# A decode block on one core: ScalarE sums the score products of 24 cache positions, and one weight load is split by partitions

## The chip, the cores and the metric

The kernel runs on one core of one Trainium2 chip. A core has a matrix engine (TensorE, in the profile PE), a vector engine (VectorE, DVE), a scalar engine (ScalarE, ACT), GpSimd (POOL), and SyncE (SP), which here issues nearly all transfers. Sixteen DMA engines move data between the chip's memory (HBM) and the core's own memory (SBUF, 128 partitions). The metric is the device time of one execution in microseconds (us), lower is better. Three runs of the kernel before took 662.41, 664.11 and 664.48 us, median 664.11.

## The reference

One decode step of a transformer block for two sequences, all inputs in bf16: layer norm of x, attention of 32 heads over a cache of 8192 keys and values of 128 numbers each, an output projection, a residual, layer norm again, and a gated ReLU feed-forward layer with a second residual.

```python
def _A_ref(x, k_cache, v_cache, wq, wo):
    q = (x @ wq) ...                                     # (B=2, 32 heads, 1, 128)
    scores = einsum("bhqd,bhkd->bhqk", q, k) * (128 ** -0.5)
    o = einsum("bhqk,bhkd->bhqd", softmax(scores), v)
    return (o as rows of 32*128) @ wo
def _B_ref(x, W_gate, W_up, W_down):
    gate = x @ W_gate; up = x @ W_up
    return ((gate * (gate > 0)) * up) @ W_down
h = A_x + _A_ref(_layernorm(A_x), A_k_cache, A_v_cache, A_wq, A_wo)
h2 = h + _B_ref(_layernorm(h), B_W_gate, B_W_up, B_W_down)
```

The two caches hold 268 MB of the 281 MB that the kernel reads. Each key and each value is used once, by one query.

## The kernel before

**Steps.** A step takes four heads of one sequence. There are 16 such groups: steps 0 to 14 (`Q` = `LASTQ` = 14 is the last full one), and the sixteenth is done as two half steps of two heads, `p0` and `p1`. The keys of a full step are one tile of 128 partitions by 32768 numbers (8 MB): 32 partitions per head, and on each partition 256 *positions* of 128 numbers. The values of a step are a tile of the same size.

**Buffers.** SBUF has three buffers of 8 MB (`bufs`). The keys of step i lie in buffer 2i mod 3, its values in the next. So the values of step i+1 are loaded into the buffer of the keys of step i, and the keys of step i+2 into the buffer of the values of step i. Keys and values alternate on SyncE's queue in the order K0, V0, K1, V1, K2 and so on, each issued when its buffer comes free; near the end the order is V12, K13, K14, V13, V14, then the half steps.

**Scores.** In a step the last `npe` positions go to TensorE (`scores_pe`, L309): it transposes them (L332), ScalarE copies the transposes back (L333), TensorE multiplies them by the query (L323), and small copies put the scores into the tile `scol` (L354). The first `nv = 256 - npe` positions go to VectorE: `products` (L358) multiplies the keys by the query in place with one instruction (L362), and `scores` (L366) halves the 128 products of each position four times by adding (L373), sums the remaining eight (L377) and takes the maximum over `scol` (L381). `npe` is 24 in steps 0 to 8, 32 in steps 9 to 13, and 16 from step 14 on (`NPE_AT`, L61).

**The rest of a step.** `largest` (L385) spreads the maxima by a TensorE product, `exponentials` (L390) takes the minimum of their negatives on VectorE (L393) and the exponentials on ScalarE (L398), and `values` (L405) multiplies 64 groups of four positions with the values on TensorE (L411); ScalarE copies the result out (L416).

**Order.** Nothing is scheduled by a tool. The program text is the order in which each engine takes its instructions, and an engine waits in that order; semaphores between engines are put in from the tiles that are read and written. In the loop (L477 to L509) a step issues `scores_pe`, `products`, `scores`, the load of the next values, `largest`, `exponentials`, then in some steps extra work, then `values` and the load of the keys after next. The extra work is `close(i - 1)` in steps 4, 8 and 12 (it divides the outputs of four finished groups by their sums, on TensorE and VectorE), and in step 12 also `lay_rows(0, ...)` (L496): two `spread` operations on VectorE (L446), two TensorE products of their results (L457) and a VectorE copy. The loads of the weights `wo`, `W_gate`, `W_up` and `W_down` come after step 14 (L519 to L561). Eight completion semaphores serve all loads in turn, so a load also waits until the load eight before it has landed.

**The tail.** After the last attention products the second layer norm and the feed-forward layer run on the weights as they land; the last instruction group is the product with `W_down` (L644), an addition, a transpose, and the 2 KB store of the result (L655).

Of the kernel before, what the change touches and what calls it, by code (L numbers as in the profile page):

```python
# [7 lines left out]
ACT = mybir.ActivationFunctionType  # L8
ALU = mybir.AluOpType
# [14 lines left out]
def kernel(  # L24
# [32 lines left out]
    VG = 4  # L57


    NPE = 32  # L60
    NPE_AT = {**{i: 24 for i in range(9)}, LASTQ: 16, LASTQ + 1: 16, LASTQ + 2: 16}  # L61
    QZ = 32


# [59 lines left out]
    class Step:  # L124
        def __init__(self, i):
            self.i = i
            self.quad = i <= LASTQ
            if self.quad:
                self.b, self.g = divmod(i, NQ)
                self.nh, self.nt = NH, TILE // Dh  # L130
                self.kt = bufs[0 if i == LASTQ else 2 * i % 3]
                self.vt = bufs[1 if i == LASTQ - 1 else (2 * i + 1) % 3]
                self.qr = qrep[:, i, :]
                self.pg, self.zc = pgq, zc[:, self.b, self.g, :]
            else:
# [8 lines left out]
            self.nv = self.nt - self.npe  # L144
            self.hp = P // self.nh

        def rows(self, j):
# [32 lines left out]
    with tc.manual_schedule():  # L180
# [123 lines left out]
            shares(i)  # L304
            normalise(i)

        scols = {}

        def scores_pe(s, between=lambda: None):  # L309


            U = s.npe // 4
            nh, nv = s.nh, s.nv
            row_ps = ps.tile([nh * U, 4 * P], f32, tag="row")

            def times_q(c0):
                for k in range(0, TPC, 4):
                    u = (c0 + k) // 4
                    if s.quad:
                        z = qz[:, QZ - NH - NH * u:QZ - NH - NH * u + NH * U]  # L320
                    else:
                        z = qzp[:, s.k, 14 - 2 * u:14 - 2 * u + 2 * U]
                    nc.tensor.matmul(  # L323
                        out=row_ps, lhsT=z, rhs=s.kt[:, (nv + c0 + k) * Dh:(nv + c0 + k + 4) * Dh],
                        start=(u == 0), stop=(u == U - 1),
                    )

            for c0 in range(0, s.npe, TPC):
                t_ps = ps2.tile([P, TPC, P], bf16, tag="tp")
                for k in range(TPC):  # L330
                    t = nv + c0 + k
# [16 lines left out]
            if s.i < Q:  # L348
                scols[s.i] = small.tile([P, s.nt], f32, tag="scol", name="scol")
            else:  # L350
                scols[s.i] = s.kt[:, (nv + 8) * Dh:(nv + 8) * Dh + 2 * s.nt].bitcast(f32)
            for j in range(nh):
                r = s.rows(j)
                nc.scalar.activation(  # L354
                    out=scols[s.i][r, nv:s.nt].rearrange("p (u t) -> p t u", t=4), in_=sc_ps[r, :, :, j], func=ACT.Copy,
                )

        def products(s, t0=0, t1=None):  # L358

            n = (s.nv if t1 is None else t1) - t0  # L360
            kv = _free(s.kt, t0 * Dh, [[Dh, n], [1, Dh]])
            nc.vector.tensor_tensor(out=kv, in0=kv, in1=_free(s.qr, 0, [[0, n], [1, Dh]]), op=ALU.mult)  # L362

        pms = {}

        def scores(s, early=lambda: None):  # L366

            scol = scols[s.i]
            width = Dh
            while width > 8:  # L370
                half = width // 2
                lo = _free(s.kt, 0, [[Dh, s.nv], [1, half]])
                nc.vector.tensor_tensor(out=lo, in0=lo, in1=_free(s.kt, half, [[Dh, s.nv], [1, half]]), op=ALU.add)  # L373
                if width == Dh:
                    early()
                width = half
            nc.vector.tensor_reduce(  # L377
                out=scol[:, 0:s.nv], in_=_free(s.kt, 0, [[Dh, s.nv], [1, 8]]), axis=AXIS.X, op=ALU.add,
            )
            pms[s.i] = small.tile([P, 1], f32, tag="pm", name="pm", bufs=2)  # L380
            nc.vector.tensor_reduce(out=pms[s.i], in_=scol, axis=AXIS.X, op=ALU.max)  # L381
# [75 lines left out]
                nc.tensor.matmul(out=or_ps[:, b, :], lhsT=sps[b], rhs=rest[r], start=True, stop=True)  # L457
            nc.vector.tensor_copy(orow[k], or_ps.rearrange("p b c -> p c b"))

        def attend_set(k):  # L460
            for c0 in range(SROWS[k]):
# [14 lines left out]
        place_q(steps[0])  # L476
        for i in range(Q):  # L477
            s = steps[i]
            scores_pe(s)
            place_q(steps[i + 1])  # L480
            products(s)
            scores(s)
            if i == Q - 2:
                load_tile(A_k_cache, steps[Q], steps[Q].kt)
            else:
                load_tile(A_v_cache, steps[i + 1], steps[i + 1].vt)
            if i == Q - 1:
                scores_pe(steps[Q])
            largest(s)
            if i == Q - 1:  # L490
                products(steps[Q], 0, steps[Q].nv // 4)
            exponentials(s)
            if i - 1 in groups:
                close(i - 1)
            if i == 12:
                lay_rows(0, [spread(0, b) for b in range(B)])  # L496
            half = s.nt // VG // 2
            values(s, 0, half)
            if i == Q - 1:
# [19 lines left out]
        for k, (h0, n, at) in enumerate(SETS):  # L519
            nc.sync.dma_start(  # L520
                out=wo[:, at * D:(at + n) * D], in_=_dram(A_wo, h0 * Dh * D, [[n * D, P], [1, n * D]]),
            )
        nc.sync.dma_start(
            out=wo[:, HM * D:(HM + 2) * D].rearrange("p (h n) -> p h n", n=D),
            in_=_dram(A_wo, HM * Dh * D, [[P // 4 * D, 4], [D, P // 4], [Dh * D, 2], [1, D]]),
        )
        nc.sync.dma_start(
            out=wo[:, (HM + 2) * D:Hq * D].rearrange("p (h n) -> p h n", n=D),
            in_=_dram(A_wo, (HM + 2) * Dh * D, [[D, P], [Dh * D, 2], [1, D]]),
# [1 line left out]
        products(p0, p0.nv // 4)  # L531

        done = [0]

        def some_values():
            if done[0] < s.nt // VG:
                values(s, done[0], done[0] + 8)
                done[0] += 8

        scores_pe(p0, some_values)  # L540
        some_values()
        load_tile(A_v_cache, p1, p1.vt, pieces=4)
        scores(p0)
# [8 lines left out]
        exponentials(p0)  # L552
        products(p1, p1.nv // 2)
        some_values()
        for w, src, c, n in ((0, B_W_gate, 0, 2), (0, B_W_gate, 2, 2), (1, B_W_up, 0, 2), (1, B_W_up, 2, 2)):
            nc.sync.dma_start(
                out=wgu[:, w, c:c + n], in_=_dram(src, c * P * F, [[F, P], [P * F, n], [1, F]]),
            )
# [127 lines left out]
```

## Time and profile before

| | |
|---|---|
| median of three runs | 664.11 us (662.41 to 664.48) |
| the profiled execution | 663.61 us, of which the span from the first to the last instruction is 661.8 us |
| DVE busy | 546.7 us (83%) |
| PE busy | 358.5 us (54%), mean granted clock 0.757 |
| ACT busy | 131.5 us (20%) |
| DMA | 281.42 MB in 8587 packets, mean 425 GB/s; busy in 39 of 40 slices at 90% or more |
| VectorE's waits for keys (L362) | 61.7 us in 15 waits, longest 5.5 us |

A busy share is an average over the run. A row "engine line op out<-in" is a group of equal instructions; "idle before, releaser" is the time in which that engine stood still ahead of them, and what ended it. SPq, ACTq are the queues of these engines, where transfers are issued. "DMA share" in a table by windows is the mean busy share of the 16 DMA engines; transfers are counted where their packets start, so a short window can show more than 1.

### The profile page before, as it was taken

Reading aid. Unit: us, or ns where it says so; the run is one execution under the profiler, and the core shown is the slowest. Engines: PE = TensorE matmul, PEld = TensorE weight load, DVE = VectorE, ACT = ScalarE, POOL = GpSimd, SP = SyncE. Lnnn points to the kernel's source line nnn. Section 1 sums busy time; section 2 is a strip of 40 time slices with the busy share of each in tenths; the row PEclk is TensorE's granted clock in tenths of the full one; section 3 lists DMA queues with packets and bytes.
Section 4 is the critical chain, followed back from the end, with each engine's and each line's share of the span. In section 5 each row is a group of like instructions: output and inputs, shape, how many; then the busy total and the mean of one; then the engine's idle time right before and its main releaser. Section 6 shows DMA issues by size and latency. Waiting matters only on the chain.

```text
span 661.8 us, 5067 instructions
## 1 busy us (share of the span) xinstructions
PE 358.5 (54%) x2143; PEld 164.7 (25%) x2143; DVE 546.7 (83%) x196; ACT 131.5 (20%) x303; POOL 5.1 (1%) x25
## 2 busy tenths in 40 slices
PE   3520843809166290835629084572928558191987
PEld 1210311304023130312204032230413224031346
DVE  2399697978969799796969979696996969999991
ACT  1120131210213121131311113131121314201410
POOL 2000000000000000000000000000000000000000
PEclk9765785958769595786959678695977869576895
DMA  9999999999999999999999999999999999999996
GB/s 380 444 441 444 440 412 421 420 428 425 436 440 405 428 433 440 440 432 409 444 432 437 444 404 437 444 429 432 432 425 440 437 440 436 417 432 426 419 418 271
DMA packets 8587, 281.42 MB, mean 425 GB/s; under 512 B 882, under 2 KB 2036, under 8 KB 3444
## 3 DMA queue, kind: packets, MB, share of 16 engines
q1 hardware_dynamic: 8560, 281.09, 98.9%
q8 instruction: 17, 0.28, 0.2%
q14 instruction: 6, 0.05, 0.0%
q10 hardware_dynamic: 4, 0.00, 0.0%
HBM read 281.09 MB, written 0.00 MB: 425 GB/s over the span
## 4 chain that ended last, share of the span: by engine, by line
DVE 40%; DMA 39%; PE 17%; ACT 2%; issue 1%; SPq 0%; DVEq 0%; ACTq 0%
DMA tile<-in_A_k_cache_dram 30%; DVE tile L362 19%; DVE tile L373 18%; PE pv_ps L411 15%; DMA tile<-in_A_wo_dram 4%; DMA tile<-in_B_W_up_dram 2%; ACT pgq L398 2%; DVE scol L377 2%; DMA tile<-in_A_wq_dram 2%; PE q_ps L241 1%; DMA tile<-in_B_W_down_dram 1%; PE mx_ps L388 1%; DVE pm L381 0%; DVE tile L377 0%; DVE nm L393 0%
## 5 line engine op out<-in xcount | busy, mean ns | idle before, releaser
L362 DVE TENSOR_TENSOR tile<-tile,qrep 128x29696 bf16<-128x29696 bf16 (+3 forms) x16 | 232.4, 14524 | 61.5 <-DMA tile<-in_A_k_cache_dram 61.5
L411 PE MATMUL pv_ps<-tile,pgq 128*16 128x512 bf16 x960 | 240.9, 417 | 43.3 <-ACT pgq L398 43.3
L373 DVE TENSOR_TENSOR tile<-tile 128x14848 bf16<-128x14848 bf16 (+7 forms) x68 | 240.2, 3532 | 2.3
L411 PEld LDWEIGHTS <-pgq 128*16 128x16 bf16 x960 | 91.2, 97 | 186.9 <-issue 45.5
L388 PE MATMUL mx_ps<-nscale,pm 128*128 128x128 f32 x34 | 12.9, 481 | 201.3 <-DVE pm L381 201.3
L398 ACT ACTIVATE pgq<-scol,nm 32x256 bf16<-32x256 f32 x56 | 28.3, 505 | 193.3 <-DVE nm L393 192.2
L388 PEld LDWEIGHTS mx_ps<-nscale,pm 128*128 128x128 f32 x34 | 8.1, 295 | 203.8 <-DVE pm L381 191.3
L333 ACT ACTIVATE tile<-t_ps 128x1024 bf16<-128x1024 bf16 x53 | 52.6, 1022 | 23.9 <-PE t_ps L332 23.4
L416 ACT ACTIVATE pv<-pv_ps 16x512 f32<-16x512 f32 (+1 forms) x16 | 9.4, 588 | 233.0 <-PE pv_ps L411 233.0
L323 PE MATMUL row_ps<-tile,qz 128*24 128x512 bf16 (+2 forms) x98 | 29.6, 383 | 18.7 <-ACT tile L333 18.6
L332 PE MATMUL t_ps<-ident,tile 128*128 128x128 bf16 x424 | 31.9, 227 | 5.6 <-DMA tile<-in_A_k_cache_dram 5.6
L332 PEld LDWEIGHTS <-tile 128*128 128x128 bf16 x424 | 25.6, 102 | 20.3 <-issue 14.4
L377 DVE TENSOR_REDUCE scol<-tile 128x232 f32<-128x1856 bf16 (+1 forms) x14 | 28.9, 2063 | 1.8 <-DVE tile L373 0.5
L362 DVE TENSOR_TENSOR tile<-tile,qpair 128x7168 bf16<-128x7168 bf16 (+2 forms) x4 | 15.5, 3884 | 0.2 <-DMA tile<-in_A_k_cache_dram 0.2
L393 DVE TENSOR_REDUCE nm<-mx_ps 128x4 f32<-128x128 f32 (+1 forms) x17 | 4.9, 291 | 12.1 <-PE mx_ps L388 12.1
L323 PEld LDWEIGHTS <-qz 128*24 128x24 bf16 (+2 forms) x98 | 7.9, 92 | 28.1 <-issue 22.7
L244 DVE CAST tile<-q_ps 2x512 bf16<-2x512 f32 x8 | 5.4, 679 | 10.6 <-PE q_ps L241 10.6
L354 ACT ACTIVATE scol<-sc_ps 32x24 f32<-32x24 f32 (+1 forms) x56 | 11.7, 210 | 8.2 <-PE sc_ps L345 7.2
L241 PE MATMUL q_ps<-tile,xn 128*2 128x512 bf16 x32 | 8.7, 429 | 8.4 <-DMA tile<-in_A_wq_dram 8.4
L345 PE MATMUL sc_ps<-ident_f,tile 24*128 24x24 f32 (+3 forms) x68 | 7.2, 220 | 11.1 <-ACT tile L341 11.1
L341 ACT ACTIVATE tile<-row_ps 24x512 f32<-24x512 f32 (+3 forms) x17 | 10.0, 586 | 13.0 <-PE row_ps L323 13.0
L398 ACT ACTIVATION_READ_ACCUMULATOR pgq<-scol,nm 32x1 f32 x56 | 10.3, 184 | 0.0
(115 smaller groups left out, 112.6 us busy)
## 6 DMA issues: line engine op xcount, KB each, us to landing
tile<-in_A_k_cache_dram SPq DMA_DIRECT2D x2, 4096.0 KB, 21.2
tile<-in_A_wq_dram SPq DMA_DIRECT2D x1, 4096.0 KB, 12.3
tile<-in_A_v_cache_dram SPq DMA_DIRECT2D x1, 4096.0 KB, 20.0
tile<-in_A_v_cache_dram SPq DMA_DIRECT2D x4, 1024.0 KB, 17.8
tile<-in_A_wo_dram SPq DMA_DIRECT2D x1, 2048.0 KB, 24.5
tile<-in_B_W_gate_dram SPq DMA_DIRECT2D x2, 688.0 KB, 14.9
tile<-in_B_W_up_dram SPq DMA_DIRECT2D x2, 688.0 KB, 16.1
tile<-in_A_wo_dram SPq DMA_DIRECT2D x1, 1024.0 KB, 26.4
```

The lines of the kernel that those rows point to most:

```text
L241: nc.tensor.matmul(out=q_ps, lhsT=xn[:, c, :], rhs=wq_sb[:, c, n0:n0 + 4 * Dh], start=(c == 0), stop=(c == KC - 1),)
L323: nc.tensor.matmul(out=row_ps, lhsT=z, rhs=s.kt[:, (nv + c0 + k) * Dh:(nv + c0 + k + 4) * Dh], start=(u == 0), stop=(u == U - 1),)
L332: nc.tensor.transpose(t_ps[:, k, :], s.kt[:, t * Dh:(t + 1) * Dh], ident)
L333: nc.scalar.activation(out=s.kt[:, (nv + c0) * Dh:(nv + c0 + TPC) * Dh], in_=t_ps.rearrange("p t s -> p (t s)"), func=ACT.Copy,)
L341: nc.scalar.activation(out=rows, in_=row_ps, func=ACT.Copy)
L354: nc.scalar.activation(out=scols[s.i][r, nv:s.nt].rearrange("p (u t) -> p t u", t=4), in_=sc_ps[r, :, :, j], func=ACT.Copy,)
L362: nc.vector.tensor_tensor(out=kv, in0=kv, in1=_free(s.qr, 0, [[0, n], [1, Dh]]), op=ALU.mult)
L373: nc.vector.tensor_tensor(out=lo, in0=lo, in1=_free(s.kt, half, [[Dh, s.nv], [1, half]]), op=ALU.add)
L377: nc.vector.tensor_reduce(out=scol[:, 0:s.nv], in_=_free(s.kt, 0, [[Dh, s.nv], [1, 8]]), axis=AXIS.X, op=ALU.add,)
L388: nc.tensor.matmul(out=mx[s.i], lhsT=_free(pms[s.i], 0, [[0, P]]), rhs=nscale, start=True, stop=True)
L398: nc.scalar.activation(out=s.pg[r, :, j, :], in_=scol[r, :].rearrange("p (u t) -> p u t", t=VG), func=ACT.Exp, scale=SCALE, bias=nm[r, j:j ...
L411: nc.tensor.matmul(out=pv_ps[s.i][r, :], lhsT=s.pg[:, u].rearrange("p j t -> p (j t)"), rhs=s.vt[:, u * VG * Dh:(u + 1) * VG * Dh], start= ...
```

## The change

Five things change in the text.

1. **Sums on ScalarE.** A new function `act_sums` takes the first `na` = 24 positions of a step (16 in `p0` and `p1`): after VectorE has multiplied them, ScalarE copies each position onto itself with an accumulated sum that goes to its place in `scol`. `scores` then halves and sums only positions `na` to `nv` on VectorE.
2. **Where it stands.** At the end of `exponentials` of step i, VectorE gets the products of the first 24 positions of step i+1 as an instruction of their own, and ScalarE the 24 sums, both ahead of `close` and `lay_rows` of step i and of the copy L416. The products of positions 24 on stay where they were. For step 0 both come ahead of the loop's first `scores_pe`. In the half step `p0` the sums are laid in pieces between the parts of `scores_pe`; those of `p1` come after `exponentials(p0)`.
3. **TensorE's share.** `npe` is 32 in step 0, 24 in steps 1 to 13, and 16 after that, as before.
4. **Weight loads.** Heads 28 and 29 of `wo` come by two loads, of partitions 0 to 123 and of 124 to 127, in place of one; `W_gate` comes by one load in place of two.
5. **Small moves.** The score tiles of step 14, `p0` and `p1` lie in `qrep` in place of the key buffer, and `attend_set(0)` is done in two parts around `diagonals(Q)` and `largest(p1)`.

```diff
-    NPE = 32
-    NPE_AT = {**{i: 24 for i in range(9)}, LASTQ: 16, LASTQ + 1: 16, LASTQ + 2: 16}
+    NPE = 24
+    NPE_AT = {0: 32, LASTQ: 16, LASTQ + 1: 16, LASTQ + 2: 16}
+    NACT = 24
+    NACT_AT = {LASTQ + 1: 16, LASTQ + 2: 16}
...
+        def act_sums(s, t0=0, t1=None):
+
+            if t0 == 0 and s.i < Q:
+                scols[s.i] = small.tile([P, s.nt], f32, tag="scol", name="scol")
+            for t in range(t0, s.na if t1 is None else t1):
+                kv = s.kt[:, t * Dh:(t + 1) * Dh]
+                nc.scalar.activation(out=kv, in_=kv, func=ACT.Copy, accum_out=scols[s.i][:, t:t + 1])
...
-                lo = _free(s.kt, 0, [[Dh, s.nv], [1, half]])
-                nc.vector.tensor_tensor(out=lo, in0=lo, in1=_free(s.kt, half, [[Dh, s.nv], [1, half]]), op=ALU.add)
+                lo = _free(s.kt, s.na * Dh, [[Dh, s.nv - s.na], [1, half]])
+                hi = _free(s.kt, s.na * Dh + half, [[Dh, s.nv - s.na], [1, half]])
+                nc.vector.tensor_tensor(out=lo, in0=lo, in1=hi, op=ALU.add)
...
             s = steps[i]
+            if i == 0:
+                products(s, 0, s.na)
+                act_sums(s)
             scores_pe(s)
             place_q(steps[i + 1])
-            products(s)
+            products(s, s.na)
             scores(s)
...
             exponentials(s)
+            if i < Q - 1:
+                products(steps[i + 1], 0, steps[i + 1].na)
+            act_sums(steps[i + 1])
             if i - 1 in groups:
                 close(i - 1)
             if i == 12:
...
-        nc.sync.dma_start(
-            out=wo[:, HM * D:(HM + 2) * D].rearrange("p (h n) -> p h n", n=D),
-            in_=_dram(A_wo, HM * Dh * D, [[P // 4 * D, 4], [D, P // 4], [Dh * D, 2], [1, D]]),
-        )
+        for r0, r1 in ((0, P - 4), (P - 4, P)):
+            nc.sync.dma_start(
+                out=wo[r0:r1, HM * D:(HM + 2) * D].rearrange("p (h n) -> p h n", n=D),
+                in_=_dram(A_wo, (HM * Dh + r0) * D, [[D, r1 - r0], [Dh * D, 2], [1, D]]),
+            )
...
-        scores_pe(p0, some_values)
+        scores_pe(p0, values_then_sums)
+        act_sums(p0, 10)
...
+        act_sums(p1)
-        for w, src, c, n in ((0, B_W_gate, 0, 2), (0, B_W_gate, 2, 2), (1, B_W_up, 0, 2), (1, B_W_up, 2, 2)):
+        for w, src, c, n in ((0, B_W_gate, 0, 4), (1, B_W_up, 0, 2), (1, B_W_up, 2, 2)):
...
-        attend_set(0)
+        attend_set(0, 0, 10)
         diagonals(Q)
         largest(p1)
+        attend_set(0, 10)
```

`values_then_sums` calls `some_values` (eight groups of `values` of step 14) and then `act_sums(p0, ...)` for positions 0 to 5, 6 and 7, and 8 and 9 in turn.

More of the change, by code (lines that the diff above doesn't have):

```diff
@@ L144, in __init__ @@
             self.nv = self.nt - self.npe
+            self.na = NACT_AT.get(i, NACT)
             self.hp = P // self.nh
@@ L305, in close @@
             normalise(i)
-        scols = {}
+        scols = {
+            i: qrep[:, c0:c0 + n].rearrange("p i d -> p (i d)").bitcast(f32)
+            for i, c0, n in ((Q, 6, 4), (Q + 1, 10, 2), (Q + 2, 12, 2))
+        }
         def scores_pe(s, between=lambda: None):
@@ L347, in scores_pe @@
                 )
[L348 to L351, printed above, removed]
             for j in range(nh):
@@ L362, in products, with scores @@
             nc.vector.tensor_tensor(out=kv, in0=kv, in1=_free(s.qr, 0, [[0, n], [1, Dh]]), op=ALU.mult)
+        def act_sums(s, t0=0, t1=None):
[4 more added lines that the diff above has]
+                nc.scalar.activation(out=kv, in_=kv, func=ACT.Copy, accum_out=scols[s.i][:, t:t + 1])
         pms = {}
-        def scores(s, early=lambda: None):
+        def scores(s):
             scol = scols[s.i]
@@ L371, in scores @@
                 half = width // 2
-                lo = _free(s.kt, 0, [[Dh, s.nv], [1, half]])
-                nc.vector.tensor_tensor(out=lo, in0=lo, in1=_free(s.kt, half, [[Dh, s.nv], [1, half]]), op=ALU.add)
-                if width == Dh:
-                    early()
+                lo = _free(s.kt, s.na * Dh, [[Dh, s.nv - s.na], [1, half]])
+                hi = _free(s.kt, s.na * Dh + half, [[Dh, s.nv - s.na], [1, half]])
+                nc.vector.tensor_tensor(out=lo, in0=lo, in1=hi, op=ALU.add)
                 width = half
             nc.vector.tensor_reduce(
-                out=scol[:, 0:s.nv], in_=_free(s.kt, 0, [[Dh, s.nv], [1, 8]]), axis=AXIS.X, op=ALU.add,
+                out=scol[:, s.na:s.nv], in_=_free(s.kt, s.na * Dh, [[Dh, s.nv - s.na], [1, 8]]), axis=AXIS.X, op=ALU.add,
             )
@@ L458, in lay_rows, with attend_set @@
             nc.vector.tensor_copy(orow[k], or_ps.rearrange("p b c -> p c b"))
-        def attend_set(k):
-            for c0 in range(SROWS[k]):
+        def attend_set(k, r0=0, r1=None):
+            for c0 in range(r0, SROWS[k] if r1 is None else r1):
                 for c in range(KC):
@@ L533, with values_then_sums @@
         done = [0]
+        parts = [0, 6, 8, 10]
+        def values_then_sums():
+            some_values()
+            k = done[0] // 8
+            act_sums(p0, parts[k - 1], parts[k])
         def some_values():
```

## Prediction

> **What bounds the kernel now.** First the page's slices, for which resource never rests.
>
> ```profile
> PE 358.5 (54%) x2143; PEld 164.7 (25%) x2143; DVE 546.7 (83%) x196; ACT 131.5 (20%) x303; POOL 5.1 (1%) x25
> DMA  9999999999999999999999999999999999999996
> ```
>
> The DMA engines do not rest until the last slice; VectorE, the busiest compute engine, has 17% free. Second, the waits, VectorE's and then SyncE's (who waited for whom: us in total, times, longest):
>
> ```profile
> DVE tile L362 <- DMA tile<-in_A_k_cache_dram: 61.7, 15, 5.5
> ...
> SPq L158 <- DVE scol L377: 278.9, 14, 39.8
> SPq L158 <- PE pv_ps L411: 277.3, 16, 20.7
> ```
>
> VectorE waits for keys in each step, so it is not the bound. But the loads are issued by what VectorE (values of the next step) and TensorE (keys after next) finish, so compute can starve the engines if it issues late. Third, whether it does: windows between landings (length, busy times, clock, DMA share, GB/s).
>
> ```profile
> 31.50:128.10 96.60, 44.01 (x216) 19.60 (x217) 84.03 (x18) 16.12 (x38) 0.00 (x0) 0.69 1.00 435
> 128.10:148.40 20.30, 3.48 (x20) 1.65 (x19) 16.63 (x7) 5.81 (x16) 0.00 (x0) 0.68 1.00 414
> 206.50:226.70 20.20, 5.28 (x41) 3.28 (x40) 18.21 (x9) 5.58 (x12) 0.00 (x0) 0.68 0.96 406
> 226.70:499.10 272.40, 147.80 (x741) 64.41 (x742) 232.12 (x59) 57.37 (x135) 0.00 (x0) 0.76 1.00 432
> ```
>
> Full speed is 435 GB/s. The stretches behind the loads of keys issued at 126.42 and 205.04 us have 414 and 406, so there the queue ran nearly dry. The packets fit: a 64 KB packet takes 2.418 us and the next starts at its end; a load of 8 MB gives each of the 16 engines eight, 19.3 us. The load issued at 126.42 has its first packet at 128.14, 1.7 us later, when most engines had just run out (128.13 to 130.03), and its first packets last 2.8 to 3.8 us. Counted by bytes at full rate, the engines lost 3.4 us between 128 and 492 us, nearly all behind issues less than 2.2 us ahead of need.
>
> Fourth, VectorE, TensorE and SyncE at the end of step 12, where the change puts an instruction (start, us, engine, line):
>
> ```profile
> 536.13 0.26 DVE L296 RECIPROCAL rz<-z_ps 128x16 f32<-128x16 f32 x1 [0.70 <-PE z_ps L292]
> 536.43 0.18 DVE L300 TENSOR_TENSOR ocol<-o_ps,rz 128x16 bf16<-128x16 f32 x1
> 536.52 0.48 DVE L446 TENSOR_TENSOR qrep<-ocol,quot 128x128 bf16<-128x128 bf16 x2
> 537.29 0.19 DVE L458 CAST orow<-or_ps 128x32 bf16<-128x32 f32 x1 [0.29 <-PE or_ps L457]
> 541.10 15.09 DVE L362 TENSOR_TENSOR tile<-tile,qrep 128x28672 bf16<-128x28672 bf16 x1 [3.62 <-DMA tile<-in_A_k_cache_dram]
> ...
> 538.04 15.69 PE L411 MATMUL pv_ps<-tile,pgq 128*16 128x512 bf16 x64 [0.79 <-ACT pgq L398]
> ...
> 553.76 0.33 SPq L158 DMA_DIRECT2D tile<-in_A_v_cache_dram  x1
> ```
>
> The extra work of step 12 is done in VectorE's wait for the keys of step 13, TensorE then runs `values(12)`, and its end issues the load V13.
>
> **The change, part by part.** *Shorter steps on VectorE.* At 232 positions (steps 1 to 8 before) the four additions and the sum take 7.89 + 4.02 + 2.09 + 1.12 + 2.09 = 17.22 us; at 224 (steps 9 to 13), 7.62 + 3.89 + 2.02 + 1.09 + 2.02 = 16.65. The slope is 71 ns a position, so 208 positions take 15.50. The products go from 15.63 (or 15.09) to 232 positions in two instructions, 1.75 + 14.02 us by the slope of the L362 rows, with 0.03 between. Keys landed to loads issued: 1.5 us less in steps 1 to 8, 0.4 less in 9 to 13. None of it is on the path by itself, since the engines are full; what it buys is part of the 3.4 us. With 1.5 us more lead the issue at 126.42 is no longer late, nor are those at 205 and 283; the three in steps 9 to 12 (0.25 us each) keep half. Bounds: 0 (the slow packets have another cause) and 4.9 (twelve steps from 72.64 to 541.10 take 39.04 us each, against 38.65 in the quiet ones from 229.59 to 306.89; some of that is instruction fetches, 16 KB packets of 0.9 us). I take -3.0, nearest to the count by packets.
>
> *Sums on ScalarE.* No row shows an accumulating copy. Nearest is the exponential with a sum, 64x128: 0.40 us and 0.18 for the accumulator read, 0.50 us from one to the next; a plain copy of 128x256 takes 0.38, the 32x256 exponential pair 0.69 without overlap. 24 sums: 7 to 17 us, I take 12. They start about 2.2 us after the keys land and end at 14.2. Behind them in ScalarE's queue stand the copy L416 (in step 1 at landing + 13.2 before) and the copies for `scores_pe`, 6.6 us. `scol` is then complete at about 21, and VectorE wants it at 29. It costs nothing; the cover of 8 us is gone only from 0.8 us a sum on. The Trainium skill ("ScalarE: Activation LUTs", Rules for kernel authors) says to use VectorE, not ScalarE, for adds. Per position the rows agree (71 ns against some 500), and by that rule alone the move would be a loss; ScalarE's 80% idle time decides otherwise.
>
> *TensorE 24 for 32 in steps 9 to 13*: one group of eight transposes and two products less, some 2 us of PE that is ready long before `scol` is wanted: 0. Step 0 with 32 issues V1 about 3 us earlier, where the queue had 4 us in hand: 0.
>
> *The products moved ahead of step i's rest.* They wait for the keys of step i+1; queued behind them on VectorE are `close` in steps 4, 8, 12, whose results nobody waits for soon, and in step 12 also the `spread`s, for which TensorE waits in `lay_rows`, with `values(12)` behind it, and V13 behind that. Before, `values(12)` starts at 538.04. Now: keys landed (541.10 in this trace's time) + 1.78 products + 0.26 + 0.18 + 0.48 with gaps + 0.4 `or_ps` = 544.1, 6.1 us later. `values` takes 15.3 to 16.7, so V13 is issued about 19.2 us after the keys are taken up: 560.3 in place of 553.76. The load ahead of it, K14, finishes on its 16 engines from 557.17 to 559.98 (median 557.7). With 1.7 us to the first packet (562.0) they idle 2.0 to 4.8 us, 4.3 at the median, and the first packets of a dry queue lose 0.6 more. The lower bound is the slowest engine's 2.6, the upper the fastest's 6.2. I take the mean, +4.9. No cover remains: V14 (573.23) is queued too late to fill in.
>
> *Instruction fetches.* ScalarE issues some 390 copies more; a handful of 0.9 us packets more on one engine each: +0.2 (0 to 1).
>
> *The `wo` heads by 124 and 4 partitions.* Before: 256 KB in 1 KB packets of 46 ns, 0.74 us on each of 16 engines. No transfer of 124 rows is in the trace. Those that are there give each engine the same number of rows (128 rows: 16 completions; the store of 8 rows: eight; x with two rows: two). If that is kept, 124 rows fit on four engines only: 62 packets, 2.85 us there, 2.1 more than before; the other twelve have 0.7 less. Bounds: 0, and 11.4 (one engine). I take four. The Trainium skill ("DMA: Bandwidth & Descriptors", Why a DMA increments its semaphore by 16 and not by 1) states it so: the largest count up to 16 that divides the slowest dimension, which for 124 is four.
>
> It matters through who ends last. Before, the engines end from 655.0 to 658.28, the last 2.0 us after the mean, because they had drifted apart. The dry queue at V13 starts all of them together again; then the four with 2.1 more end last, with 0.5 of scatter 2.6 after the mean: +0.6 (-0.8 if the load is spread evenly).
>
> *`W_gate` in one load, one load more for `wo`*: each load waits for the one eight before, which shifts by one; at each such wait 4 to 5 MB (10 us) are still queued: 0. *Score tiles in `qrep`, `attend_set(0)` in two parts, 16 sums in `p0` and `p1`*: they ease waits of 1 to 3 us in a stretch whose end waits for weights: 0. The 3.5 us from the last data to the end stay.
>
> Sum: -3.0 + 4.9 + 0.2 + 0.6 = +2.7 us. The profiled execution took 663.61, giving 666.3; the median stands 0.5 above it, giving 666.6 when half of that is added.
>
> **The rivals.** *A: the late V13 hardly counts (faster).* If the slowest engine sets the end, it loses only 2.6 at V13, and could win back up to 4.9 before it; with an even `wo`: 664.1 - 2.3 = 661.8. It decides if `values(12)` ends within 17 us of the keys' arrival, or if the four engines are not last. For it: keys land when the slowest engine is done. Against: after a common start the four have 2.1 us more to do.
> *B: even (no change).* The gain of 3.0 against a loss of 4.9, with the `wo` heads spread evenly: +1.3, or a gain nearer 4.9: +0.8; 664.9 to 665.4.
> *C: nothing is won early (slower still).* The slow packets behind 126 and 205 us have a cause other than a late issue: +2.7 + 3.0 = 669.8. Against it: behind the loads issued at least 2.7 us ahead of need there are almost none. (ScalarE's sums would be worse: at 1.0 us each `scol` is 5 us late in every step, more than the queue's lead of about 4.)
>
> **How the numbers follow.** About 0.3% (2.0 us) is what a measurement can tell from no change. The forecast (665.5 to 669) has 48%, A 18%, B 24%, C 10%. Slower by over 0.3% (above 666.1) takes most of the forecast and C: 0.56; within 0.3% B and the forecast's lower edge: 0.26; faster: 0.18. The range 661.6 to 670.5 holds A's centre, B, the forecast and C's centre, with some of their far sides left out.
>
> **What would show it.** In step 12 `values` starts about 3 us after VectorE takes up the keys of step 13, and V13 is issued some 19 us after; a window behind it shows a DMA share well under 1. The windows behind the third and fifth keys show 434 and not 414 and 406. L362 has a 128x3072 row of 1.75 us, ScalarE's sums cost near 0.5 us, and VectorE's wait for keys grows from 5.5 to about 7 us in steps 1 to 8. At the end a few engines carry the 1 KB packets of `wo` longer than the rest. The prediction is wrong if V13's delay is refilled, if the slow windows stay, or if the sums hold up `scol`.

## The result and the profile after

The changed kernel took 665.70 us (median of six runs, 665.04 to 667.16) against 662.39 for the kernel before in the same session (660.91 to 664.48): a ratio of 1.0049, with a 95% interval of 1.0027 to 1.0071, or +3.3 us (1.8 to 4.7). Run again beside the experiments the ratio was 1.0055 (1.0036 to 1.0074). The forecast was +2.7 us, and 666.6 from a median of 664.11 before. The profiled execution after took 665.04 us, of which the span is 663.2. Over 31 runs the kernel before has a median of 662.05, so its profiled execution (663.61) was one of its slower ones.

First the page of the kernel after, busy times and DMA slices.

```profile
PE 359.2 (54%) x2103; PEld 164.0 (25%) x2103; DVE 524.0 (79%) x210; ACT 243.6 (37%) x1083; POOL 5.1 (1%) x25
DMA  9999999999999999999999999999999998999997
```

VectorE has lost 22.7 us of work (546.7 before), ScalarE has gained 112 us (131.5), and the program is slower. The DMA slices show where to look: one slice of 16.6 us, the 34th, from 547 to 564 us, is under 9. Who waits for whom, VectorE's row first and then SyncE's:

```profile
DVE tile L364 <- DMA tile<-in_A_k_cache_dram: 83.9, 15, 7.9
```

```profile
SPq L161 <- PE pv_ps L420: 280.8, 16, 24.8
SPq L161 <- DVE scol L386: 267.5, 14, 35.9
```

VectorE waits longer for keys (61.7 us before), SyncE less for VectorE (278.9). SyncE's longest wait for TensorE, though, went from 20.7 to 24.8 us: that one is for the load V13. The windows, with the same limits as before and one added behind the keys of step 13 (length, busy times of PE, PEld, DVE, ACT and POOL, clock, DMA share, GB/s):

```profile
31.50:128.10 96.60, 48.69 (x238) 21.52 (x239) 79.94 (x21) 39.47 (x184) 0.00 (x0) 0.68 1.00 432
128.10:148.40 20.30, 3.90 (x15) 1.56 (x14) 14.73 (x7) 4.84 (x15) 0.00 (x0) 0.58 1.06 456
206.50:226.70 20.20, 5.05 (x17) 2.33 (x17) 13.72 (x7) 4.28 (x15) 0.00 (x0) 0.58 1.00 435
226.70:499.10 272.40, 146.42 (x712) 62.99 (x710) 224.15 (x67) 102.58 (x462) 0.00 (x0) 0.76 1.00 433
```

```profile
545.00:575.00 30.00, 19.62 (x114) 9.12 (x112) 29.66 (x8) 10.81 (x34) 0.00 (x0) 0.83 0.89 374
```

The two slow windows (414 and 406 GB/s before) are gone; 456 is more than full speed only because packets are counted where they start. The new hole is in the last row: a DMA share of 0.89, where the kernel before has 1.03 and 444 GB/s. What made it, at the end of step 12 (start, us, engine, line; in brackets the idle time before and what ended it), and SyncE's issue of V13:

```profile
538.44 1.76 DVE L364 TENSOR_TENSOR tile<-tile,qrep 128x3072 bf16<-128x3072 bf16 x1 [5.43 <-DMA tile<-in_A_k_cache_dram]
...
540.50 0.48 DVE L455 TENSOR_TENSOR qrep<-ocol,quot 128x128 bf16<-128x128 bf16 x2
...
540.84 0.39 PE L466 MATMUL or_ps<-rest,qrep 128*128 128x16 bf16 x2 [7.16 <-DVE qrep L455]
...
541.16 15.45 PE L420 MATMUL pv_ps<-tile,pgq 128*16 128x512 bf16 x64
```

```profile
556.64 0.33 SPq L161 DMA_DIRECT2D tile<-in_A_v_cache_dram  x1
```

The early products come first, `spread` and the two small products follow, `values` starts 2.7 us after the keys are taken up, and V13 is issued 18.2 us after (553.76 before, with keys that were taken up 2.7 us later than here).

The groups of the new instructions (count, busy us, mean ns):

```profile
L372 ACT ACTIVATE tile<-tile 128x128 bf16<-128x128 bf16 x392 | 114.8, 294 | 72.6 <-DVE tile L364 72.5
L372 ACT ACTIVATION_READ_ACCUMULATOR tile<-tile 128x1 f32 x392 | 73.0, 186 | 0.0
...
L364 DVE TENSOR_TENSOR tile<-tile,qrep 128x3072 bf16<-128x3072 bf16 x14 | 24.6, 1758 | 79.8 <-DMA tile<-in_A_k_cache_dram 79.8
```

Last, SyncE's queue in the stretch of the weights:

```profile
606.19 25.83 SPq L539 DMA_DIRECT2D tile<-in_A_wo_dram x2
632.06 0.55 SPq L543 DMA_DIRECT2D tile<-in_A_wo_dram  x1
632.72 3.07 SPq L161 DMA_DIRECT2D tile<-in_A_v_cache_dram  x4
637.12 0.38 SPq L580 DMA_DIRECT2D tile<-in_B_W_gate_dram  x1
```

Issuing the two split `wo` loads took 25.8 us. The issue of the load of 124 rows took 0.4; that of the load of *four* rows, 8 KB, held SyncE from 606.6 to 632.0. Behind it in the queue stood the last `wo` load and four pieces of the last values, which the kernel before issues between 613.5 and 633.

### The profile page after: what moved, and what is told of

The parts are those of the page before. It is cut to its first block, busy times and chain, and to the rows that moved or that the text cites. A ratio compares the mean times of both kernels' runs of the same rounds, so it can differ in the third digit from the quotient of the medians.

```text
span 663.2 us, 5777 instructions
## 1 busy us (share of the span) xinstructions
PE 359.2 (54%) x2103; PEld 164.0 (25%) x2103; DVE 524.0 (79%) x210; ACT 243.6 (37%) x1083; POOL 5.1 (1%) x25
## 4 chain that ended last, share of the span: by engine, by line
DMA 40%; DVE 39%; PE 17%; ACT 2%; issue 1%; SPq 0%; DVEq 0%; ACTq 0%
DMA tile<-in_A_k_cache_dram 30%; DVE tile L364 19%; DVE tile L384 17%; PE pv_ps L420 15%; DMA tile<-in_A_wo_dram 5%; DMA tile<-in_B_W_up_dram 2%; ACT pgq L407 2%; DVE scol L386 2%; DMA tile<-in_A_wq_dram 2%; PE q_ps L244 1%; DMA tile<-in_B_W_down_dram 1%; PE mx_ps L397 1%; DVE pm L390 0%; DVE nm L402 0%; DVE qrep L386 0%
## 5 line engine op out<-in xcount | busy, mean ns | idle before, releaser
L364 DVE TENSOR_TENSOR tile<-tile,qrep 128x3072 bf16<-128x3072 bf16 (+4 forms) x30 | 235.7, 7887 | 79.8 <-DMA tile<-in_A_k_cache_dram 79.8
L384 DVE TENSOR_TENSOR tile<-tile 128x13312 bf16<-128x13312 bf16 (+7 forms) x68 | 217.7, 3202 | 2.3
L372 ACT ACTIVATE tile<-tile 128x128 bf16<-128x128 bf16 x392 | 114.8, 294 | 72.6 <-DVE tile L364 72.5
L372 ACT ACTIVATION_READ_ACCUMULATOR tile<-tile 128x1 f32 x392 | 73.0, 186 | 0.0
L339 ACT ACTIVATE tile<-t_ps 128x1024 bf16<-128x1024 bf16 x49 | 48.5, 1021 | 14.3 <-PE t_ps L338 14.0
L329 PE MATMUL row_ps<-tile,qz 128*24 128x512 bf16 (+2 forms) x90 | 28.4, 398 | 26.4 <-ACT tile L339 26.4
L338 PE MATMUL t_ps<-ident,tile 128*128 128x128 bf16 x392 | 30.1, 231 | 7.8 <-DMA tile<-in_A_k_cache_dram 7.8
L338 PEld LDWEIGHTS <-tile 128*128 128x128 bf16 x392 | 24.2, 104 | 21.6 <-issue 13.3
L386 DVE TENSOR_REDUCE scol<-tile 128x208 f32<-128x1664 bf16 (+1 forms) x14 | 26.3, 1882 | 1.4
```

The costliest lines, as they stand in the source:

```text
L329: nc.tensor.matmul(out=row_ps, lhsT=z, rhs=s.kt[:, (nv + c0 + k) * Dh:(nv + c0 + k + 4) * Dh], start=(u == 0), stop=(u == U - 1),)
L339: nc.scalar.activation(out=s.kt[:, (nv + c0) * Dh:(nv + c0 + TPC) * Dh], in_=t_ps.rearrange("p t s -> p (t s)"), func=ACT.Copy,)
L372: nc.scalar.activation(out=kv, in_=kv, func=ACT.Copy, accum_out=scols[s.i][:, t:t + 1])
L384: nc.vector.tensor_tensor(out=lo, in0=lo, in1=hi, op=ALU.add)
L386: nc.vector.tensor_reduce(out=scol[:, s.na:s.nv], in_=_free(s.kt, s.na * Dh, [[Dh, s.nv - s.na], [1, 8]]), axis=AXIS.X, op=ALU.add,)
```

## The experiments

The theory after the first comparison: the change wins some 3 us ahead of step 13 and gives back more in two places that have nothing to do with the sums, the late V13 and SyncE's stop at the small load. The rivals: the sums on ScalarE cost something themselves; only one of the two places counts.

A count is used below that is taken from the trace's DMA records: the *lost time* of a stretch is its length less the bytes moved in it at full rate (16 engines, one 64 KB packet each in 2.414 us from start to start), so it counts both engines that stand still and packets that last longer. All columns are us, of one profiled execution each; "V14 landed" is the last of that load's 16 completions. Second executions of `after` and `both` landed V14 at 599.5 and 597.1, so a difference of less than 1 us in that column says little.

| kernel | lost, 130 to 545 | lost, 545 to 575 | V14 landed | from there to the last data |
|---|---|---|---|---|
| before | 3.6 | 0.1 | 598.6 | 59.7 |
| after | 0.9 | 3.4 | 598.7 | 61.0 |
| `order` | 0.8 | 0.6 | 596.6 | 63.5 |
| `wo_one` | 1.2 | 4.2 | 599.7 | 59.2 |
| `both` | 0.9 | 0.3 | 596.4 | 59.9 |
| `b_wait` | 2.3 | 4.0 | 600.2 | 59.4 |
| `b_split` | 4.3 | 0.1 | 598.3 | 61.0 |
| `wo_112` | 1.0 | 0.3 | 596.5 | 60.8 |
| `wo_120` | 1.0 | 0.7 | 597.0 | 61.1 |
| `no_sums` | 0.7 | 0.1 | 594.9 | 59.3 |
| `long_copies` | 0.7 | 0.0 | 595.1 | 59.2 |
| `mix` | 1.2 | 0.1 | 595.4 | 59.3 |

The first column sorts the kernels by VectorE's steps: the three with the steps of the kernel before lose 2.3 to 4.3 us there, the nine with shorter steps 0.7 to 1.2.

**The kernel after once more (`a_again`).** No edit.

> The changed kernel itself, to stand beside the others on the same chip. All theories: 3.3 us above the kernel before (665.7 against 662.4), with the load V13 issued about 20 us after the keys of step 13 land, and one load of four rows of wo holding SyncE for some 25 us.

665.79 us, ratio 1.0055 (1.0036 to 1.0074). Its profile has the same two marks: V13 issued at 557.48, SyncE held for 26.4 us by the load of four rows.

**V13 on time (`order`).** In step 12 alone the early products and the sums move behind `close` and `lay_rows`.

```diff
-            if i < Q - 1:
-                products(steps[i + 1], 0, steps[i + 1].na)
-            act_sums(steps[i + 1])
+            if i != 12:
+                if i < Q - 1:
+                    products(steps[i + 1], 0, steps[i + 1].na)
+                act_sums(steps[i + 1])
...
+                products(steps[i + 1], 0, steps[i + 1].na)
+                act_sums(steps[i + 1])
```

> In step 12 alone, close and lay_rows come first and the early products and sums of step 13 after them; all else as changed. Theory 1 (the late V13 is the larger loss, 3.3 us by bytes counted in the trace): V13 is issued about 14 us after the keys of step 13 land and the DMA engines do not go idle there; 3 us less than the changed kernel, so level with the kernel before, -0.5 to +1. Theory 2 (ScalarE's sums or their instruction fetches cost the time): no change from the changed kernel, +3. Theory 3 (the end is set by the split load of wo alone): at most 1 us less than the changed kernel.

665.33 us, ratio 1.0044 (1.0026 to 1.0062): nearly nothing is won, where the first theory expected the time of the kernel before. The timeline of step 12 in `order` shows that the edit did what it should, and SyncE's queue what stood against it.

```profile
535.50 16.76 PE L420 MATMUL pv_ps<-tile,pgq 128*16 128x512 bf16 x64 [0.78 <-ACT pgq L407]
...
538.34 15.69 DVE L364 TENSOR_TENSOR tile<-tile,qrep 128x3072 bf16<-128x3072 bf16 x2 [3.40 <-DMA tile<-in_A_k_cache_dram]
...
552.29 0.33 SPq L161 DMA_DIRECT2D tile<-in_A_v_cache_dram  x1
```

```profile
604.81 26.59 SPq L542 DMA_DIRECT2D tile<-in_A_wo_dram  x2
631.45 0.72 SPq L546 DMA_DIRECT2D tile<-in_A_wo_dram  x1
632.28 2.80 SPq L161 DMA_DIRECT2D tile<-in_A_v_cache_dram  x4
```

V13 is issued 4.3 us earlier than in the kernel after, the hole behind it is gone (0.6 us lost in place of 3.4) and V14 has landed at 596.6 and not 598.7. But SyncE comes free at the same time as before, so transfers that are now 2 us further on find an empty queue: from V14 to the last data it takes 63.5 us in place of 61.0, and an engine stands still for 3.5 us of that on the mean, in place of 0.8.

**One `wo` load (`wo_one`).** The kernel after, with heads 28 and 29 of `wo` in one load as in the kernel before.

```diff
-        for r0, r1 in ((0, P - 4), (P - 4, P)):
-            nc.sync.dma_start(
-                out=wo[r0:r1, HM * D:(HM + 2) * D].rearrange("p (h n) -> p h n", n=D),
-                in_=_dram(A_wo, (HM * Dh + r0) * D, [[D, r1 - r0], [Dh * D, 2], [1, D]]),
-            )
+        nc.sync.dma_start(
+            out=wo[:, HM * D:(HM + 2) * D].rearrange("p (h n) -> p h n", n=D),
+            in_=_dram(A_wo, HM * Dh * D, [[P // 4 * D, 4], [D, P // 4], [Dh * D, 2], [1, D]]),
+        )
```

> Heads 28 and 29 of wo come by one load of 128 rows again; the order of step 12 stays as changed. Theory 1: the stop of SyncE for 25 us goes, with it the slow stretch from 632 to 640 us (355 GB/s against 418, 1.2 us), and the four engines that end late: 1 to 2 us less than the changed kernel, +1.5 to +2 over the kernel before. Theory 3: all of the loss goes, level with the kernel before. Theory 2: no change.

664.30 us, ratio 1.0028 (1.0011 to 1.0045), 1.5 us less than the kernel after in the same session. The issue takes 0.46 us, and the last column of the table falls from 61.0 to 59.2. V13 is still late (4.2 us lost).

**Both edits (`both`).** `order` with the one `wo` load.

> Both of these: the order of step 12 mended, and wo by one load of 128 rows. Theory 1: what is left is the gain of shorter VectorE steps, 3.1 us by bytes in the profiled runs: 1.5 to 3 us below the kernel before, and no issue of keys or values less than 3 us ahead of need. Theory 2: +3. Theory 3: as the run with one load of wo.

661.79 us (661.65 to 662.24), ratio 0.9987 (0.9972 to 1.0002); run again as `both_again` 661.93, 0.9996 (0.9982 to 1.0009). The two losses are gone, but so is most of the gain of 1.5 to 3 us that was expected to be left: `no_sums` below looks for it.

> The kernel with the order of step 12 mended and one load of wo, to stand beside the next three on the same chip: 661.8, 0.1% below before, spread under 1 us. One of the 16 engines, the one that fetches most of ScalarE's instructions, ends each load about 1.7 us after the next slowest.

The two edits give 0.5 us and 1.5 us alone and 4.0 together. Either of the two marks half hides the other. The windows 632 to 636 and 636 to 640 of `order`, then of `both`:

```profile
632.00:636.00 4.00, 4.00 (x21) 1.61 (x19) 4.00 (x3) 4.00 (x29) 0.00 (x0) 1.00 0.93 323
636.00:640.00 4.00, 4.00 (x58) 2.53 (x57) 3.86 (x5) 0.97 (x4) 0.00 (x0) 1.00 1.02 364
```

```profile
632.00:636.00 4.00, 4.00 (x20) 1.59 (x19) 3.97 (x4) 4.00 (x28) 0.00 (x0) 1.00 1.05 427
636.00:640.00 4.00, 3.92 (x57) 2.57 (x55) 3.90 (x4) 0.62 (x2) 0.00 (x0) 1.00 1.01 429
```

**Each mark alone, put into the kernel before (`b_wait`, `b_split`).** `b_wait` is the kernel before with the products of 24 positions of step 13 ahead of `close` and `lay_rows` in step 12, and nothing else; `b_split` is the kernel before with the `wo` loads of 124 and 4 rows.

```diff
-            products(s)
+            products(s, 24 if i == 13 else 0)
...
+            if i == 12:
+                products(steps[i + 1], 0, 24)
             if i - 1 in groups:
                 close(i - 1)
```

> The kernel before with one edit: in step 12 the products of the first 24 positions of step 13 are put ahead of close and lay_rows, as the change has them; no sums on ScalarE, wo unchanged. Theory 1 (a late V13 costs by itself): V13 is issued 19 to 20 us after the keys of step 13 land, the engines lose 3.3 to 4.9 us there by bytes, and the run is 2.5 to 4.5 us slower than before. Theory 2 (the sums cost it): no change, within 0.5.

> The kernel before with one edit: heads 28 and 29 of wo by loads of 124 and 4 rows. Theory 1: the load of four rows holds SyncE until some 631 us, the pieces of the last values are issued after it, and since nothing else is late the queue runs dry for longer than in the changed kernel: 2.5 to 4 us slower. If the cost is only that four engines have 2.1 us more to move: 0 to 1.5 slower and no stop of SyncE.

`b_wait`: 665.0 us, ratio 1.0036 (1.0018 to 1.0055), +2.4 us; 4.0 us are lost from 545 to 575, 3.4 in the kernel after. `b_split`: 664.56 us, ratio 1.0026 (1.0008 to 1.0044), +1.7 us, less than the 2.5 to 4 expected; SyncE is held for 21.5 us, and V14 has landed at 598.3, as in the kernel before (598.6). So each mark costs time without the rest of the change.

**Other splits (`wo_112`, `wo_120`).** `order` with loads of 112 and 16, or of 120 and 8 rows, in place of 124 and 4.

```diff
-        for r0, r1 in ((0, P - 4), (P - 4, P)):
+        for r0, r1 in ((0, P - 16), (P - 16, P)):
```

> The kernel with the order of step 12 mended, and the two heads of wo by loads of 112 and 16 rows in place of 124 and 4: as many loads, but both numbers divide by 16. Theory 1 (124 rows go to four engines, and their full queues stop SyncE): no stop, all engines alike, level with the kernel that has one load (661.8, 0.3 below before). Rival (one load more in the turn of the eight semaphores makes the later loads wait): as with 124 and 4, 665.3, 3 above before.

> The order of step 12 mended, and the two heads of wo by loads of 120 and 8 rows. Both numbers divide by 8 and not by 16. Theory 1 (rows go to as many engines as divide them, and a full queue on these stops SyncE): the first load lies on eight engines with 30 packets each, SyncE is held for a shorter time or not at all, and the time lies between the runs with 112 and 16 (662.9) and with 124 and 4 (665.3): 662.9 to 664. If any number that 16 does not divide is as bad: 665.3.

662.87 us, 1.0003 (0.9989 to 1.0017), and 663.24 us, 1.001 (0.9995 to 1.0025): 2.5 and 2.1 us less than with 124 and 4 rows, 1.1 and 1.3 more than `both` in one load. SyncE is not stopped in either. In `wo_112`:

```profile
604.81 0.95 SPq L542 DMA_DIRECT2D tile<-in_A_wo_dram  x2
```

How many DMA engines a load uses can be read from the page's count of small packets, since every engine of a load ends with a write of 4 bytes. The packet lines of the kernel after, of `both`, of `wo_112` and of `wo_120`:

```profile
DMA packets 8568, 281.45 MB, mean 424 GB/s; under 512 B 858, under 2 KB 2012, under 8 KB 3420
```

```profile
DMA packets 8576, 281.45 MB, mean 427 GB/s; under 512 B 866, under 2 KB 2020, under 8 KB 3428
```

```profile
DMA packets 8592, 281.45 MB, mean 426 GB/s; under 512 B 882, under 2 KB 2036, under 8 KB 3444
```

```profile
DMA packets 8583, 281.45 MB, mean 425 GB/s; under 512 B 873, under 2 KB 2027, under 8 KB 3435
```

`both` has 866 with one load on 16 engines, so 850 without it. 124 and 4 rows add 8 (4 + 4), 112 and 16 rows add 32 (16 + 16), 120 and 8 rows add 23 (15 + 8). The Trainium skill ("DMA: Bandwidth & Descriptors", Why a DMA increments its semaphore by 16 and not by 1) gives the number of engines as the largest count up to 16 that divides the slowest dimension, and the counts of all three pairs agree (for 120 rows it is 15, where the expectation for `wo_120` had taken eight). So only the pair on four engines stops SyncE; a load of 8 rows right behind one of 120 does not.

What 112 and 16 rows still cost is another thing: one load more in the turn of the eight semaphores. SyncE's waits in `both` and in `wo_112`:

```profile
SPq L161 <- DMA tile<-in_A_wo_dram: 1.8, 1, 1.8
...
SPq L161 <- DMA tile<-in_A_k_cache_dram: 1.7, 2, 0.9
```

```profile
SPq L161 <- DMA tile<-in_A_k_cache_dram: 9.3, 1, 9.3
...
SPq L161 <- DMA tile<-in_A_wo_dram: 7.6, 2, 4.6
```

Each piece of the last values (L161) waits for a load one later in the turn. The last piece is issued at 635.0 where `both` issues it at 631.5, and the window from 632 to 636 has 360 GB/s in place of 427. The engines do not stand still longer for it: between V14 and the last data it is 1.7 us on the mean, 1.8 in `both`. What grows is the time of the packets of 8, 4 and 1 KB, by 0.9 us an engine; packets of 1 KB, 46 ns each in `both`, take 53 to 60 ns from 631 to 635 us. The split in the kernel after shows the same: beside `wo_one`, 1.1 us an engine in longer packets and 0.6 in standing still. Whether the later issue or the other shape of the load makes the packets longer was not tried apart.

**The sums left out (`no_sums`).** `both`, where one ScalarE copy lays the first product of each of the 24 positions into `scol` in place of the 24 sums: the scores of these positions are not computed. All other work is done.

```diff
-            for t in range(t0, s.na if t1 is None else t1):
-                kv = s.kt[:, t * Dh:(t + 1) * Dh]
-                nc.scalar.activation(out=kv, in_=kv, func=ACT.Copy, accum_out=scols[s.i][:, t:t + 1])
+            e = s.na if t1 is None else t1
+            kv = _free(s.kt, t0 * Dh, [[Dh, e - t0]])
+            nc.scalar.activation(out=scols[s.i][:, t0:e], in_=kv, func=ACT.Copy)
```

> The kernel with both edits undone (661.8), but with the 24 sums left out: one copy of 24 numbers takes their place on ScalarE, so the scores of these positions are not the reference's. Theory 1 (the sums lie under the transfers): within 0.5 of 661.8. Theory 2: the sums, or the fetches of their instructions, cost 1 us or more, and it is at 660.8 or below.

659.66 us (659.55 to 660.31), ratio 0.9952 (0.9936 to 0.9968). The sums thus cost 2.1 us against `both`, though `scol` is complete in time in both and the lost time up to 545 us is nearly the same (0.9 and 0.7 us). The page's DMA queues of `both`, and of `no_sums` with ScalarE's group:

```profile
q14 instruction: 12, 0.10, 0.0%
```

```profile
q14 instruction: 6, 0.05, 0.0%
...
L372 ACT ACTIVATE scol<-tile 128x24 f32<-128x24 bf16 x14 | 3.4, 244 | 72.2 <-DVE tile L364 72.2
```

Queue 14 fetches ScalarE's instructions: its packets go from 12 to 6 with ScalarE's instructions (1140 in `both`, 376 in `no_sums`). The trace's packets do not name their DMA engine, but while the engines are full a packet starts 3 to 4 ns before the end of the one ahead of it, so the packets can be strung together into 16 engines. In the trace of `both` the fetches at 118.8, 194.3, 272.2, 350.1, 420.7, 484.1 and 547.5 us (8 KB each) then all lie on one engine. Each takes 0.31 us, and the data packet behind it 2.72 in place of 2.42, so the engine falls back by 0.6 us each time, 4.2 in all. It is the last to complete V14, at 596.43, with the next at 594.97 (the 16 KB fetches of queue 8 are spread over many of the other engines). In `no_sums` no engine has more than three of ScalarE's fetches, and the last completes V14 at 594.94. A load counts as landed when its slowest engine is done, so a loss that the mean hardly shows counts here: V14 lands 1.5 us later than in `no_sums` in `both`, and 2.1 in `both_again`.

**The same work in few instructions (`long_copies`).** `both`, with the sums replaced by four copies of all 24 positions onto themselves and the one copy of `no_sums`; the scores of these positions are not computed here either. ScalarE is busy for longer than with the sums, in 454 instructions.

```diff
+            kv = s.kt[:, t0 * Dh:e * Dh]
+            for _ in range(4):
+                nc.scalar.activation(out=kv, in_=kv, func=ACT.Copy)
```

> The same, but in place of the 24 sums ScalarE copies the same 24 positions onto themselves four times in one instruction each (about 2.7 us each, 11 in all), and copies 24 numbers in place of the scores, so these scores are not the reference's. As much work and memory traffic on ScalarE, a sixth of its instructions or less. Theory 1 (the sums cost 2 us because their instructions are fetched through one DMA engine, which then ends last): 659.7, as without sums. Rival (ScalarE's work itself, or its memory traffic, slows the transfers or the end): 661.8.

660.46 us, ratio 0.997 (0.9952 to 0.9988), 1.5 us less than `both_again` beside it and 0.8 more than `no_sums`. ScalarE's group, and the chain that ended last, in which the copies for `p1` stand close to the end:

```profile
L373 ACT ACTIVATE tile<-tile 128x3072 bf16<-128x3072 bf16 (+3 forms) x80 | 183.6, 2295 | 74.0 <-DVE tile L364 72.0
```

```profile
631.15 1.92 ACT tile L373
633.10 1.92 ACT tile L373
635.04 1.92 ACT tile L373
636.98 1.92 ACT tile L373
```

The transfers went as in `no_sums` (V14 landed at 595.1, the last data at 654.3 against 654.2 us), with seven fetches of ScalarE's and no more than three on an engine. Of the 0.7 us by which the span is longer, 0.6 lie behind the last data: the chain that ends last runs through these long copies and not through the weights. So ScalarE's 184 us of work on the key buffers cost the transfers nothing, and what costs goes with the number of instructions. That it does so through the one engine with seven fetches is read from the traces; no run sent the same fetches to several engines.

**Fewer sums (`mix`).** `both` with 8 sums on ScalarE and 32 positions on TensorE in steps 0 to 13.

```diff
-    NPE = 24
-    NPE_AT = {0: 32, LASTQ: 16, LASTQ + 1: 16, LASTQ + 2: 16}
-    NACT = 24
+    NPE = 32
+    NPE_AT = {LASTQ: 16, LASTQ + 1: 16, LASTQ + 2: 16}
+    NACT = 8
```

> The same as the first, with 32 positions on TensorE and 8 sums on ScalarE in steps 0 to 13: VectorE then works about as much less in steps 1 to 8 as with 24 sums (1.6 us less than before), with a third of the sums. If the lead at the issues and the instruction fetches are what counts: 660 to 661, 0.2 to 0.35% below before, and better than both kernels.

659.87 us (659.56 to 660.33), ratio 0.996 (0.9946 to 0.9975): 2.1 us less than `both_again` and, of the kernels that compute everything, the only one that beats the kernel before beyond its interval. ScalarE has 673 instructions and eight fetches, the last completion of V14 is at 595.4, and VectorE's steps are still 8 to 16 positions shorter than before.

## Why the prediction was right, and where its terms were not

The direction and the size were right (+2.7 forecast, +3.3 measured). By single terms, though, one that was too large stood beside two that were too small. A chain of kernels, each of which differs from the last by one part, prices them by medians: before to `no_sums` -2.8 us (by the ratio -3.2, interval 2.1 to 4.2), `no_sums` to `both` +2.1, `both` to `wo_one` +2.5, `wo_one` to after +1.5. They add up to +3.3; the median of the kernel before moved by up to 0.4 us between sessions. That the errors cancel is luck in part. In part it is not: the two middle terms overlap, as said below, and together they are 4.6 us where the prediction has 5.1.

- *Shorter steps on VectorE, -3.0: right.* The lost time from 130 to 545 us fell from 3.6 to 0.9, the two slow windows are gone, and all that the change brings without the sums, the late V13 and the split is -2.8 to -3.2. TensorE's share, `W_gate` in one load and the small moves are in this figure and were not taken apart. VectorE's wait for keys, predicted to grow by 1.5 us in steps 1 to 8, went from 4.3 to 5.8 on the mean. Rival C falls with this. (The upper bound of 4.9 is 4.7 by its own figures, 12 times 0.39.)
- *Sums on ScalarE, 0 for their time: right, and safer than thought.* They come every 0.29 us, not 0.5: the accumulator read of 0.19 runs beside the next copy. 24 of them end 7 us after they start, not 12.
- *The late V13, +4.9: the mechanism is right, the size is not.* Every mark was there: `values` 2.7 us after the keys (about 3 predicted), V13 issued 18.2 us after (19.2), a DMA share of 0.89 behind it. The cost is 2.5 us (`wo_one` against `both`) and 2.4 (`b_wait`, 1.2 to 3.7). The step that failed is "I take the mean, +4.9". The mean itself was too large: the engines lost 3.4 to 4.2 us, since V13 was issued 1.0 us sooner than reckoned and its first packet came 1.0 us after the issue and not 1.7. And what follows waits for the slowest engine. In `b_wait` the last engine is done with K14 at 557.9 and V13's first packets start at 559.2 to 559.7, and last some 0.7 us longer than usual: 2.0 to 2.5 us lost. A dry queue also lines the engines up again: V13's completions lie 0.7 us apart in the kernel after and 3.7 apart in `both`. The lower bound, the slowest engine's 2.6, was the better choice. That half of rival A was right.
- *Instruction fetches, +0.2: the term that was sized worst.* In place of "a handful of 0.9 us packets more on one engine each" came six more packets that each cost their engine 0.6 us, seven of the twelve on one engine, and 2.1 us. In the kernel after this engine ends K14 at 557.97, 1.6 us behind the next, and goes straight on to V13, for which the other 15 have stood still: the late V13 and the fetches hide each other in part. So the 2.1 and the 2.5 us hold in this order of the chain; the sums were not taken out of the kernel after, and how the 4.6 us divide there is open.
- *The `wo` split, +0.6: right that it costs and that four engines carry it, wrong in how.* The price is 1.5 us in the kernel after, 1.7 in `b_split` and 3.5 with V13 on time (`order` against `both`). The longer packets on four engines were priced; that the issue of the next load on these engines would hold SyncE for 25 us, with five loads behind it in the queue, was not foreseen.
- *`wo`'s extra load, 0: wrong once V13 is on time.* The shift by one in the turn of the semaphores goes with 1.1 us in `wo_112`. That enough is still queued at each such wait did not hold for the small pieces of the last values: they were issued 3.5 us later, and the packets around them lasted longer.
- *Rival A* had the net effect the other way: its cheap V13 was real, but the fetches and SyncE's stop took more than the -2.3 us it counted on. *Rival B's* even spread of the `wo` heads did not happen. *The 3.5 us from the last data to the end* stayed (3.5 us in both profiles).

## What to carry to other kernels

Where the DMA engines never rest, price a late load by the slowest engine and not by the mean, and look at what lines the engines up or pulls one of them back: 392 sums, seven of whose instruction fetches fall on one engine, cost more here (2.1 us) than longer work in few instructions (0.8). Keep a load in one piece where that is possible, give it a number of rows that sixteen divides, and read SyncE's timeline for long issues, since a load of 8 KB can stop everything behind it. Mend two faults before judging either: alone the mended order gave 0.5 us and the mended load 1.5, together 4.0.

## What the runs showed of the hardware that was not expected

- The issue of a transfer can block its queue without any semaphore: the load of four rows behind one of 124 held SyncE for 21.5 to 26.4 us in four traces. It began between 605 and 610 us and ended between 631.2 and 633.0 in all of them, which fits an end set by the work queued ahead better than a fixed time. Loads of 8 rows behind 120 and of 16 behind 112 did not do it. Why four engines do was not tried.
- An instruction fetch of 8 KB costs its DMA engine 0.6 us: 0.31 of its own, and 0.30 more on the next data packet. Seven such fetches, spread over 430 us, fell on the same engine and left it 1.5 us behind the next.
- Packets behind a dry queue last longer: the first 64 KB packets of the late V13 took 2.8 to 3.4 us in the kernel after, in place of 2.42.
- The kernel before scatters over 6.0 us in 31 runs (660.43 to 666.43); `both` and `mix` scatter over 0.6 and 0.8 us in twelve. That their earlier issues are the reason was not tried.
